# Fewer and larger loads in a windowed attention and feed-forward kernel, in a fixed order ahead of the first ones

## The chip, the cores and the metric

The kernel runs on one core of one Trainium2 chip. The metric is the device time of one execution, in microseconds (us); before the change it is 712.51 us, the median of three runs.

## The reference

Attention with 4 sink keys and a window of 128 keys, over 4 batches, 8 heads, 768 positions and 64 features a head, then a feed-forward layer from 512 to 2048 and back to 512 on all 3072 tokens. Cut to what matters:

```python
scores = np.matmul(q, k.transpose(0, 1, 3, 2)) / np.sqrt(D)
keep = is_sink | in_window                    # 4 sink keys, 128 keys of window
scores = np.where(keep, scores, -1e9)
a = np.exp(scores - scores.max(-1, keepdims=True))
a = a / (a.sum(-1, keepdims=True) + 1e-9)
x = np.matmul(a, v)                           # heads side by side: 3072 x 512
h = x @ w_in                                  # 512 -> 2048
g = np.where(h >= 1, h, np.where(h <= -1, 0.0, (h + 1) ** 2 / 4))
return g @ w_out                              # 2048 -> 512
```

The weights are 64-bit floats in memory and are decoded in the kernel from their integer words.

## The kernel before, in words

A **unit** is one head of one batch and one half of its positions (three tiles of 128 queries), 64 units in all; a **chunk** is 8 units, the rows for which a feed-forward step has 384 tokens. Chunks 0 to 3 are the first halves, 4 to 7 the second halves.

The first 16 units (two chunks) are worked as 8 **pairs** of two heads in plain 32-bit matmuls. Pair `m` has `pair_load` (L389: keys, L396, and queries, L397, by two DMAs), `pair_values` (L400: for each of two heads one DMA for its values, L404, and one for its 4 sink values, L405, into a tile `vq` that was set to zero before, L634), `pair_scores` (L412: products on PE, masked minimum on DVE, L433, exponentials on ACT, L438), `pair_sums` (L441), `early_transp` (L449), `pair_r` (L479) and `pair_av` (L463: probabilities times values on PE, L474, the scaling on DVE, L477).

The other 48 units are **split units**: queries, keys, probabilities and values are split into a rounded high part and a rest. `load` (L247 on) brings keys into `k_r` (L256) and queries into `r` (L258); ACT rounds them (L259, L262), DVE, for units 16 to 19 POOL, takes the keys' rest (L261), POOL the queries' rest `q_l` (L263). `values` (L305 on) brings a unit's values into `r` as well (L310), and its sinks into `vs_r` (L316). `r`, `k_r` and `vs_r` have one buffer each, so that queries and values take turns in `r`. `scores` ends with a small POOL step, `stat` (L289), that the row sums need.

**Order.** PE's instructions run in the order in which they are written. On the other engines and on SP's queue, from which most loads are issued, a planner that simulates the program chooses the order, except where `queue(i, on)` ties an instruction behind the one queued before it on its engine; `tc.issue_after(ins)` ties what is issued in its block behind `ins` on the engine of `ins`. Neither makes an engine wait for another. `first_pairs` (L504) writes out the first five pairs: loads of pairs 0 and 1, values of pair 0, then for each pair `m` the load of pair `m + 1`, the values of pair `m` and, after the sums of pairs 0 to 3, the fetch and the decoding of a block of weights (`weights`, L186 on; 1 MB a block; blocks 0 to 3 from SP, L199, the others from ACT's queue). A decoding is four DVE steps (L164, L170, L173, L177) and one ACT step (L174), written between the next pair's steps, and `queue` holds this order on DVE and ACT. The feed-forward of chunk 0 follows, with the other 12 blocks' decoding and pairs 5 to 7 spread over it; after that each chunk's feed-forward (`stage1`, L566, and `stage2`, L585) has the next chunk's attention spread over it.

Of the kernel before, what the change touches and what calls it, by code (L numbers as in the profile page):

```python
# [1 line left out]

# [6 lines left out]
F32 = mybir.dt.float32  # L9
F32R = mybir.dt.float32r  # L10
# [5 lines left out]
B, H, S, D = 4, 8, 768, 64  # L16
DM, DFF = 512, 2048
P = 128
NT = S // P
CT = 3  # L20
NSINK = 4
KB = P + NSINK
NCT = DM // P
QK = CT * P + P + CT * KB
# [13 lines left out]
SYNC = 4  # L38
# [11 lines left out]
def attn_ffn(ctx, tc, qk, qkp, vx, vs, par, w_in, w_out, out):  # L50
    nc = tc.nc
# [12 lines left out]
    def queue(i, on=True):  # L64
        if on:
            e = i.ins.engine
            if e in queued:
                tc.add_manual_dep(i.ins, queued[e].name, mybir.DependencyInfo(
                    mybir.DependencyClass.NoSync, mybir.DependencyReason.DATA), reason="queue")
            queued[e] = i.ins  # L70
        return i
# [57 lines left out]
    with tc.issue_after(behind):  # L129
        tsel = const.tile([44, CT], F32, name="tsel")  # L130
        nc.gpsimd.memset(tsel, 0.0)
        for r0 in (0, 32):
            r = r0 + CT * NSINK
# [16 lines left out]
    raw = {}  # L150
# [7 lines left out]
    def decode_parts(t, w, words, pin=False, on=False):  # L158

        low, x = words[..., 0], words[..., 1]  # L160
        high, rest = (t[:, :, 0], t[:, :, 1]) if len(t.shape) == 4 else (t[:, 0], t[:, 1])

        def shift():
            first = nc.vector.tensor_scalar(w, x, 3, 0x3FFFFFFF, op0=ALU.logical_shift_left, op1=ALU.bitwise_and)  # L164
            if pin:
                tc.keep_in_program_order(first)
            queue(first, on)

        def sign():
            queue(nc.vector.scalar_tensor_tensor(w, x, -0x40000000, w, op0=ALU.bitwise_and, op1=ALU.bitwise_or), on)  # L170

        def tail():
            queue(nc.vector.scalar_tensor_tensor(w, low, 29, w, op0=ALU.logical_shift_right, op1=ALU.bitwise_or), on)  # L173
            queue(nc.scalar.copy(high, w.bitcast(F32)), on)  # L174

        def rest_of():
            queue(nc.vector.tensor_tensor(rest, w.bitcast(F32), high.bitcast(F32), op=ALU.subtract), on)  # L177

        return shift, sign, tail, rest_of
# [6 lines left out]
    loaded = []  # L186

    def weights(n):

        def src(k):  # L190
            return (w_in, w_out)[k % 2][k // 2 * 2:k // 2 * 2 + 2].bitcast(I32).rearrange("j p c -> p j c")

        def fetch():
            for k in range(n, min(n + min(AHEAD if n > 2 else 1, NP // 2 - n // 2 - 1) + 1, NP)):
                if k not in raw:
                    raw[k] = wpool.tile([P, 2, 2 * DM], I32, name="w")

                    with tc.issue_after(loaded[-1]) if k < SYNC else nullcontext():
                        (nc.sync if k < SYNC else nc.scalar).dma_start(raw[k], src(k))  # L199

        def parts(on):
            j, i = n // 2 * 2, n % 2
            words = raw[n].rearrange("p j (c two) -> p j c two", two=2)
            if i:
                t = wpool.tile([P, 2, 2, DM], F32R, name="w")
                w_o[j:j + 2] = t[:, 0], t[:, 1]
            else:
                t = wi2[n // 2]
            return decode_parts(t, dec.tile([P, 2, DM], I32, name=f"bits{n % 2}"), words, pin=not on, on=on)

        def f():
            fetch()
            for g in parts(False):
                g()

        if n < WFIRST:
            return fetch, lambda: parts(True)
        return f
# [24 lines left out]
    att1 = fast.enter_context(tc.tile_pool(name="att1", bufs=1))  # L243
    att = fast.enter_context(tc.tile_pool(name="att", bufs=2))
    fast.enter_context(tc.manual_schedule(engines={mybir.EngineType.PE}))
    st = {}

    def load(u):
        b, h, t0 = u
        T = CT * P  # L250
        W = (P if t0 else -NSINK) + CT * KB
        q_l = att.tile([P, T], F32R, name="q_l")
        q_h = att.tile([P, T], F32R, name="q_h")
        k_r = att1.tile([P, P + CT * KB], F32, name="k_r")[:, :W]
        k_s = att.tile([P, P + CT * KB], F32R, name="k_s")[:, :W]
        nc.sync.dma_start(k_r, qk[b, h, t0 // CT, :, T:T + W])  # L256
        q_r = att1.tile([P, T], F32, name="r")
        nc.sync.dma_start(q_r, qk[b, h, t0 // CT, :, :T])  # L258
        nc.scalar.copy(k_s, k_r)  # L259
        eng = nc.gpsimd if units.index(u) in KL_POOL else nc.vector  # L260
        eng.tensor_tensor(k_s[D:P], k_r[D:P], k_s[D:P].bitcast(F32), op=ALU.subtract)  # L261
        nc.scalar.copy(q_h, q_r)  # L262
        nc.gpsimd.tensor_tensor(q_l, q_r, q_h.bitcast(F32), op=ALU.subtract)  # L263
        st["qk", u] = ((q_h, q_l), k_s)
# [40 lines left out]
    def values(u):  # L305
        b, h, t0 = u
        kb0 = max(t0 - 1, 0)
        nb = t0 + CT - kb0
        v_r = att1.tile([P, 4, D], F32, name="r")[:, :nb]
        nc.sync.dma_start(v_r, vx[b, h, :, kb0:kb0 + nb])  # L310
        v_s = att.tile([P, 4, 2, D], F32R, name="v_s")[:, :nb]
        i, j = h % 2, 1 - h % 2
        nc.scalar.copy(v_s[:, :, i, :], v_r)
        nc.gpsimd.tensor_tensor(v_s[:, :, j, :], v_r, v_s[:, :, i, :].bitcast(F32), op=ALU.subtract)
        vs_r = att1.tile([44, D], F32, name="vs_r")
        nc.sync.dma_start(vs_r, vs[b, h])  # L316
        vs_s = vsx[units.index(u) % 2]
        nc.scalar.copy(vs_s[0:44, i, :], vs_r)
        nc.gpsimd.tensor_tensor(vs_s[0:44, j, :], vs_r, vs_s[0:44, i, :].bitcast(F32), op=ALU.subtract)
        st["v", u] = (v_s, vs_s)  # L320
# [68 lines left out]
    def pair_load(m):  # L389

        b, h, _ = units[2 * m]
        T = CT * P
        W = CT * KB - NSINK
        q_s = att.tile([P, T], F32R, name="q_h").bitcast(F32)
        k_s = att.tile([P, P + CT * KB], F32R, name="k_s").bitcast(F32)[:, :W]
        loaded.append(nc.sync.dma_start(k_s, qkp[b, h // 2, :, T:T + W]).ins)  # L396
        nc.sync.dma_start(q_s, qkp[b, h // 2, :, 0:T])  # L397
        st["qk", m] = q_s, k_s

    def pair_values(m):  # L400
        v_s = vq[m % 2]
        for a in range(2):
            b, h, _ = units[2 * m + a]
            nc.sync.dma_start(v_s[:, :CT, a], vx[b, h, :, :CT])  # L404
            nc.sync.dma_start(v_s[:NSINK, CT, a], vs[b, h, :NSINK])  # L405

    def early_p(u):

# [54 lines left out]
    def pair_av(m):  # L463

        T = CT * P
        v_s = vq[m % 2]
        ps = ps_a.tile([P, 512], F32, name="ps_a")

        terms = [(2, 4, 1, 2), (0, 0, 2, 0), (1, 2, 2, 1), None]
        for n, t in enumerate(terms):  # L470
            for a in range(2):
                k, s0, ns, i = t or (CT, 0, 1, CT - 1)
                rhs = pt0[a][:, s0 * P:(s0 + ns) * P] if t else spn[a]
                nc.tensor.matmul(ps[a * D:a * D + D, i * P:(i + ns) * P], lhsT=v_s[:, k, a], rhs=rhs,  # L474
                                 start=(n == 0), stop=(n == len(terms) - 1))
        x = xn[:, units[2 * m][1] // 2, :]
        return lambda: queue(nc.vector.tensor_tensor(x, ps[:, :T], x, op=ALU.mult), m < H // 2)  # L477
# [63 lines left out]
    units = [(b, h, t0) for b, t0 in chunks for h in range(H)]  # L541

    def attn_steps(n):
        us = {k: units[n - k] for k in (-1, 0, 1, 2) if 0 <= n - k < len(units)}
        steps = []
        if n == NATIVE:
            steps.append((0.0, lambda: load(us[0])))
        if -1 in us:
            steps.append((0.0, lambda: load(us[-1])))
        if 1 in us and n - 1 >= NATIVE:  # L550
            steps.append((0.0, lambda: values(us[1])))
        steps += [(0.22, lambda i=i: scores(us[0], i)) for i in range(CT) if 0 in us]
        steps += [(0.43, lambda: transp(us[1]))] if 1 in us and n - 1 >= NATIVE else []
        steps += [(1.0, lambda: av(us[2]))] if 2 in us and n - 2 >= NATIVE else []
        if n in CHECK:
            steps.append((0.0, lambda: recheck(n - CHECK[0], n)))
        return steps
# [70 lines left out]

    early = ExitStack()
    dec = early.enter_context(tc.tile_pool(name="dec", bufs=1))  # L630
    vq = [dec.tile([P, CT + 1, 2, D], F32, name=f"vq{i}") for i in range(2)]
    spn = [dec.tile([P, P], F32, name=f"spn{i}") for i in range(2)]
    for t in vq + spn:
        nc.vector.memset(t, 0.0)  # L634
    p0 = [att.tile([P, CT, 260], F32, name="p").rearrange("p i c -> p (i c)") for _ in range(2)]
    pt0 = [att.tile([P, 2, CT, 2, P], F32R, name="pt").bitcast(F32).rearrange("p a i c q -> p (a i c q)")
# [4 lines left out]
    for c in range(len(chunks)):  # L641
# [12 lines left out]
        b, t0 = chunks[c]  # L654
# [17 lines left out]
    ps = ps_a.tile([P, 512], F32, name="ps_a")  # L672
# [56 lines left out]
    with tc.If(other_v > 0):  # L729
        with tc.tile_pool(name="gen", bufs=1) as gen:  # L730

            for n in range(2 * NJ):
# [3 lines left out]
                m = gen.tile([P, DM], F32, name="m")  # L736
# [3 lines left out]
            for t0 in (0, CT):  # L740
                keep = gen.tile([P, CT, S], F32, name="keep")
                kidx = gen.tile([P, S], I32, name="kidx")
                r = gen.tile([P, S], F32, name="r")
                for i in range(CT):
                    m = keep[:, i]
# [53 lines left out]
```

## Time and profile before

| | before |
|---|---|
| time, median of 3 runs | 712.51 us (712.22 to 712.81) |
| the profiled execution's own time | 713.94 us |
| its span, first to last instruction | 712.2 us |
| mean granted clock of TensorE | 0.994 |
| busy PE, DVE, ACT, POOL | 688.1, 512.9, 489.4, 296.2 us |

The span is what the trace covers; the time has what lies around it too, and an execution under the profiler is a little longer than the median. PE is TensorE's matmuls, PEld its weight loads, DVE VectorE, ACT ScalarE, POOL GpSimd, SP the engine that issues most DMAs. A busy PE counts matmuls whose ends are modelled, so a stretch in which PE is full by this count can still have it waiting a little.

### The profile page before, as it was taken

The numbers are of one execution on the slowest core, as the hardware profiler recorded it, in microseconds if no ns is written. First come the engines' busy times: TensorE is split into PE (matmuls) and PEld (weight loads), VectorE is DVE, ScalarE is ACT, GpSimd is POOL, SyncE is SP. The second block draws the span as 40 slices with busy tenths as digits, with TensorE's granted clock in tenths as the row PEclk, the third lists the DMA queues.
The fourth block names the chain that finished last, engine by engine and source line by source line (L and its number), as shares of the span: only waits on it lengthen the run. The fifth ranks groups of instructions, "written<-read, shape, count | busy, mean of one in ns | idle before, by whom it ended". The sixth has DMA issues, their size and how long they took to land.

```text
span 712.2 us, 12391 instructions
## 1 busy us (share of the span) xinstructions
PE 688.1 (97%) x3937; PEld 611.2 (86%) x3937; DVE 512.9 (72%) x1405; ACT 489.4 (69%) x1265; POOL 296.2 (42%) x509
## 2 busy tenths in 40 slices
PE   6799998999999999999999999999999999999996
PEld 4577877999999999999899898999989999989995
DVE  7978998886767768788777778778776777632221
ACT  5876666686768777786777777777766866544332
POOL 2012444754544554456564455636554444400000
PEclk9999999999999999999999999999999999999999
DMA  8845533132144333254433443334422220001001
GB/s 266 297 159 188 177 126 102 46 103 58 50 138 136 104 111 120 73 165 128 118 99 108 118 126 118 118 119 123 123 56 60 88 60 17 8 1 46 0 1 49
DMA packets 44841, 73.04 MB, mean 103 GB/s; under 512 B 13024, under 2 KB 29408, under 8 KB 44768
## 3 DMA queue, kind: packets, MB, share of 16 engines
q1 hardware_dynamic: 41504, 59.59, 27.5%
q10 hardware_dynamic: 3264, 12.58, 4.9%
q8 instruction: 33, 0.54, 0.3%
q14 instruction: 40, 0.33, 0.1%
HBM read 65.87 MB, written 6.29 MB: 101 GB/s over the span
## 4 chain that ended last, share of the span: by engine, by line
PE 73%; DVE 11%; ACT 6%; DMA 3%; POOL 2%; issue 2%; SPq 0%; ACTq 0%; POOLq 0%; DVEq 0%
PE o_ps L585 30%; PE h_ps L566 30%; PE ps_a L383 4%; PE ps_a L277 4%; PE ps_a L336 2%; DVE bits L170 1%; DMA again<-w_in 1%; DVE bits L173 1%; DVE p L298 1%; ACT p L284 1%; DMA w<-w_in 1%; DVE g L575 1%; DVE gl L577 1%; POOL q_l L263 1%; PE ps_a L474 1%
## 5 line engine op out<-in xcount | busy, mean ns | idle before, releaser
L566 PE MATMUL h_ps<-x,wi 128*128 128x384 f32 x1536 | 310.5, 341 | 0.0
L566 PEld LDWEIGHTS h_ps<-x,wi 128*128 128x128 f32 x1536 | 264.3, 189 | 9.8 <-issue 1.5
L585 PE MATMUL o_ps<-w,gh 128*128 128x512 f32 x768 | 243.9, 398 | 0.0
L585 PE MATMUL o_ps<-w,gl 128*128 128x512 f32 x384 | 151.2, 394 | 0.9 <-DVE gl L577 0.9
L585 PEld LDWEIGHTS o_ps<-w,gh 128*128 128x128 f32 x768 | 134.1, 188 | 16.5 <-issue 1.7
L575 DVE SCALAR_TENSOR_TENSOR g<-g,h_ps 128x384 f32<-128x384 f32 x128 | 70.4, 550 | 63.9 <-ACT g L574 62.2
L573 ACT ACTIVATE g<-h_ps,half 128x384 f32<-128x384 f32 x128 | 73.9, 578 | 58.0 <-PE h_ps L566 56.9
L263 POOL TENSOR_TENSOR q_l<-r,q_h 128x384 fp32r<-128x384 f32 x48 | 50.7, 1056 | 132.1 <-ACT q_h L262 123.2
L576 ACT CAST gh<-g 128x384 fp32r<-128x384 f32 x128 | 65.6, 512 | 57.3 <-DVE g L575 56.8
L585 PEld LDWEIGHTS o_ps<-w,gl 128*128 128x128 f32 x384 | 72.0, 188 | 18.6 <-DVE gl L577 1.3
L577 DVE TENSOR_TENSOR gl<-g,gh 128x384 fp32r<-128x384 f32 x112 | 68.6, 612 | 25.3 <-ACT gh L576 24.3
L284 ACT ACTIVATE p<-p,peak 128x260 f32<-128x260 f32 (+1 forms) x144 | 71.4, 496 | 17.5 <-DVE peak L281 16.8
L261 DVE TENSOR_TENSOR k_s<-k_r,k_s 64x524 fp32r<-64x524 f32 (+1 forms) x44 | 46.4, 1054 | 40.0 <-ACT k_s L259 39.9
L574 ACT ACTIVATE g<-g 128x384 f32<-128x384 f32 x128 | 66.9, 523 | 2.1
L281 DVE CUSTOM_DVE_ANT_0 p<-ps_a,m 128x260 f32<-128x260 f32 (+1 forms) x144 | 56.6, 409 | 15.9 <-PE ps_a L277 15.1
L347 POOL TENSOR_SCALAR_AFFINE_SELECT pt<-pt 128x384 fp32r<-128x384 f32 (+1 forms) x96 | 51.0, 531 | 18.2 <-DVE pt L340 16.3
L298 DVE CUSTOM_DVE_ANT_0 p<-p,stat 128x128 f32<-128x128 f32 x128 | 55.4, 477 | 0.0
L345 POOL TENSOR_SCALAR_AFFINE_SELECT pt<-pt 128x384 fp32r<-128x384 f32 (+1 forms) x96 | 50.4, 525 | 7.1 <-ACT pt L339 3.0
L577 POOL TENSOR_TENSOR gl<-g,gh 128x384 fp32r<-128x384 f32 x16 | 22.6, 1415 | 69.0 <-ACT gh L576 65.5
L383 PEld LDWEIGHTS ps_a<-pt,v_s 128*128 128x128 f32 x304 | 46.6, 188 | 2.2
L383 PE MATMUL ps_a<-pt,v_s 128*128 128x256 f32 (+1 forms) x304 | 47.0, 275 | 0.0
L277 PE MATMUL ps_a<-k_s,q_h 128*128 128x260 f32 (+1 forms) x144 | 40.0, 278 | 0.9 <-DVE sk L342 0.9
(147 smaller groups left out, 977.2 us busy)
## 6 DMA issues: line engine op xcount, KB each, us to landing
r<-qk SPq DMA_DIRECT2D x48, 192.0 KB
k_r<-qk SPq DMA_DIRECT2D x32, 262.0 KB
again<-w_in SPq DMA_DIRECT2D x16, 512.0 KB
again<-w_out SPq DMA_DIRECT2D x16, 512.0 KB
w<-w_in ACTq DMA_DIRECT2D x6, 1024.0 KB
w<-w_out ACTq DMA_DIRECT2D x6, 1024.0 KB
out<-o SPq DMA_DIRECT2D x23, 256.0 KB
r<-vx SPq DMA_DIRECT2D x32, 128.0 KB
```

Source lines behind the costliest of these rows:

```text
L263: nc.gpsimd.tensor_tensor(q_l, q_r, q_h.bitcast(F32), op=ALU.subtract)
L277: nc.tensor.matmul(ps[:, lo:260], lhsT=q[:, i * P:(i + 1) * P], rhs=k_s[:, c0:c0 + 260 - lo], start=(j == 0), stop=(j == len(qs) - 1))
L284: nc.scalar.activation(p[:, i, lo:260], p[:, i, lo:260], AF.Exp, bias=peak_i, scale=-1.0, accum_out=stat[:, i:i + 1])
L298: nc.vector.tensor_tensor_reduce(out=own, in0=own, in1=p[:, i, 0:P], scale=r, scalar=0.0, op0=ALU.add, op1=ALU.add, accum_out=stat[:, i:i ...
L383: nc.tensor.matmul(z, lhsT=w, rhs=y, start=(n == 0), stop=(n == len(mms) - 1))
L566: nc.tensor.matmul(h_ps[:, :T], lhsT=w_i[j][:, w, ct * P:(ct + 1) * P], rhs=x[:, y, ct], start=(ct == 0 and n == 0), stop=(ct == NCT - 1 a ...
L573: nc.scalar.activation(g, h_ps[:, :T], AF.Relu, bias=half, scale=0.5)
L574: nc.scalar.activation(g, g, AF.Square)
L575: nc.vector.scalar_tensor_tensor(g, g, 1.0, h_ps[:, :T], op0=ALU.min, op1=ALU.max)
L576: nc.scalar.copy(gh, g)
L577: (nc.gpsimd if row0 == GL_POOL else nc.vector).tensor_tensor(gl, g, gh.bitcast(F32), op=ALU.subtract)
L585: nc.tensor.matmul(o_ps[tt], lhsT=gg[:, tt * P:(tt + 1) * P], rhs=w_o[j][:, w], start=(j == 0 and n == 0), stop=(j == NJ - 1 and n == 2))
```

## The change

A pair's queries and keys come in one DMA into one tile `qk_s`, and its two heads' values in one DMA into `vq`, whose layout is now head, tile, feature; `vq` has no place for sinks, is not set to zero, and the sinks' product takes the first tile of keys with probabilities that are zero but for four rows. A split unit's queries and keys come in one DMA into one tile `qk_r`, and its values have a tile `v_r` of their own. The pairs' loads and the first four weight blocks' are tied one behind the other on SP's queue (pairs 0 to 5), and a split unit's loads are tied behind the last pair's load that was written before them. The matmuls, their sizes and all other arithmetic stay.

```diff
-                    with tc.issue_after(loaded[-1]) if k < SYNC else nullcontext():
-                        (nc.sync if k < SYNC else nc.scalar).dma_start(raw[k], src(k))
+                    queue((nc.sync if k < SYNC else nc.scalar).dma_start(raw[k], src(k)), k < SYNC)
...
-        q_h = att.tile([P, T], F32R, name="q_h")
-        k_r = att1.tile([P, P + CT * KB], F32, name="k_r")[:, :W]
-        k_s = att.tile([P, P + CT * KB], F32R, name="k_s")[:, :W]
-        nc.sync.dma_start(k_r, qk[b, h, t0 // CT, :, T:T + W])
-        q_r = att1.tile([P, T], F32, name="r")
-        nc.sync.dma_start(q_r, qk[b, h, t0 // CT, :, :T])
+        qk_r = att1.tile([P, QK], F32, name="qk_r")[:, :T + W]
+        qk_s = att.tile([P, QK], F32R, name="qk_s")[:, :T + W]
+        with tc.issue_after(loaded[-1]):
+            nc.sync.dma_start(qk_r, qk[b, h, t0 // CT, :, :T + W])
+        q_r, k_r = qk_r[:, :T], qk_r[:, T:]
+        q_h, k_s = qk_s[:, :T], qk_s[:, T:]
...
-        v_r = att1.tile([P, 4, D], F32, name="r")[:, :nb]
-        nc.sync.dma_start(v_r, vx[b, h, :, kb0:kb0 + nb])
+        v_r = att1.tile([P, 4, D], F32, name="v_r")[:, :nb]
+        with tc.issue_after(loaded[-1]):
+            nc.sync.dma_start(v_r, vx[b, h, :, kb0:kb0 + nb])
...
-        nc.sync.dma_start(vs_r, vs[b, h])
+        with tc.issue_after(loaded[-1]):
+            nc.sync.dma_start(vs_r, vs[b, h])
...
-        q_s = att.tile([P, T], F32R, name="q_h").bitcast(F32)
-        k_s = att.tile([P, P + CT * KB], F32R, name="k_s").bitcast(F32)[:, :W]
-        loaded.append(nc.sync.dma_start(k_s, qkp[b, h // 2, :, T:T + W]).ins)
-        nc.sync.dma_start(q_s, qkp[b, h // 2, :, 0:T])
-        st["qk", m] = q_s, k_s
+        qk_s = att.tile([P, QK], F32R, name="qk_s").bitcast(F32)[:, :T + W]
+        loaded.append(queue(nc.sync.dma_start(qk_s, qkp[b, h // 2, :, :T + W]), m < H // 2 + 2).ins)
+        st["qk", m] = qk_s[:, :T], qk_s[:, T:]
...
-        for a in range(2):
-            b, h, _ = units[2 * m + a]
-            nc.sync.dma_start(v_s[:, :CT, a], vx[b, h, :, :CT])
-            nc.sync.dma_start(v_s[:NSINK, CT, a], vs[b, h, :NSINK])
+        b, h, _ = units[2 * m]
+        queue(nc.sync.dma_start(v_s, vx[b, h:h + 2, :, :CT].rearrange("a p t d -> p a t d")), m < H // 2 + 2)
...
-                k, s0, ns, i = t or (CT, 0, 1, CT - 1)
+                k, s0, ns, i = t or (0, 0, 1, CT - 1)
-                nc.tensor.matmul(ps[a * D:a * D + D, i * P:(i + ns) * P], lhsT=v_s[:, k, a], rhs=rhs,
+                nc.tensor.matmul(ps[a * D:a * D + D, i * P:(i + ns) * P], lhsT=v_s[:, a, k], rhs=rhs,
...
-    vq = [dec.tile([P, CT + 1, 2, D], F32, name=f"vq{i}") for i in range(2)]
+    vq = [dec.tile([P, 2, CT, D], F32, name=f"vq{i}") for i in range(2)]
-    for t in vq + spn:
+    for t in spn:
         nc.vector.memset(t, 0.0)
```

## Rows read from the trace of the kernel before

**Rows 1.** The page, part 1: busy us (share of the span) xinstructions of each engine.

```profile
PE 688.1 (97%) x3937; PEld 611.2 (86%) x3937; DVE 512.9 (72%) x1405; ACT 489.4 (69%) x1265; POOL 296.2 (42%) x509
```

**Rows 2.** The chain of work that ended last, in order of time, in the stretch 0 to 18 us: start us, us, what.

```profile
2.63 0.20 DVE x L106
2.83 0.13 DVE x L108
...
3.04 0.13 DVE x L115
...
4.94 6.29 DMA w<-w_in
```

**Rows 3.** The timeline of SP's queue, 0 to 60 us: start us, us, queue, line, operation, out<-in, count. The last row is the second half of the last pair's load.

```profile
1.24 0.42 SPq L396 DMA_DIRECT2D k_s<-qkp  x1
1.71 0.42 SPq L397 DMA_DIRECT2D q_h<-qkp  x1
...
59.96 0.57 SPq L397 DMA_DIRECT2D q_h<-qkp  x1
```

**Rows 4.** The page, part 6 (DMA issues: out<-in, queue, operation, count, KB each), asked for in full.

```profile
w<-w_in SPq DMA_DIRECT2D x2, 1024.0 KB
...
k_s<-qkp SPq DMA_DIRECT2D x8, 196.0 KB
q_h<-qkp SPq DMA_DIRECT2D x8, 192.0 KB
vq<-vx SPq DMA_DIRECT2D x16, 96.0 KB
```

**Rows 5.** Stretches of one us each: us, then busy time of PE, PEld, DVE, ACT, POOL (instructions), granted clock, mean busy share of the 16 DMA engines, GB/s.

```profile
6.00:7.00 1.00, 1.00 (x8) 0.56 (x4) 1.00 (x5) 0.86 (x4) 0.89 (x6) 1.00 0.88 118
7.00:8.00 1.00, 0.77 (x3) 0.18 (x1) 1.00 (x7) 0.28 (x1) 0.87 (x6) 1.00 0.90 340
```

**Rows 6.** The timeline of DVE, 0 to 18 us: start us, us, engine, line, operation, out<-in, shapes, count, and in brackets the idle time before it and what ended it.

```profile
0.96 1.03 DVE L634 MEMSET vq<- 128x512 f32 x2 [0.96 <-PEq L792]
...
10.05 0.19 DVE L446 RECIPROCAL stat<-stat 128x6 f32<-128x6 f32 x1
11.25 0.69 DVE L164 TENSOR_SCALAR bits<-w 128x1024 int32<-128x1024 int32 x1 [1.01 <-DMA w<-w_in]
...
13.54 0.42 DVE L433 CUSTOM_DVE_ANT_0 pt<-o_ps,m1n 128x260 f32<-128x260 f32 x1
...
14.24 1.22 DVE L173 SCALAR_TENSOR_TENSOR bits<-w,bits 128x1024 int32<-128x1024 int32 x1
```

**Rows 7.** The timeline of PE, 0 to 18 us, in the columns of group 6.

```profile
4.83 1.20 PE L422 MATMUL o_ps<-k_s,q_h 64*128 64x128 f32 x5 [4.83 <-DMA q_h<-qkp]
...
11.48 1.23 PE L422 MATMUL o_ps<-k_s,q_h 64*128 64x128 f32 x5
...
12.51 0.64 PE L422 MATMUL o_ps<-k_s,q_h 64*128 64x260 f32 x1
...
12.95 0.64 PE L422 MATMUL ps_a<-k_s,q_h 64*128 64x260 f32 x1
```

**Rows 8.** The chain of waits again, in the stretch 30 to 135 us: two pairs' last small products, and the first split units.

```profile
34.92 1.48 PE ps_a L486 x12
36.40 2.17 PE ps_a L474 x16
...
106.72 0.81 PE ps_a L486 x12
...
110.14 1.45 PE ps_a L474 x16
...
119.72 1.03 POOL k_s L261
...
120.82 0.24 POOL stat L289
...
124.02 3.36 PE h_ps L566 x12
...
129.46 2.08 PE h_ps L566 x12
```

**Rows 9.** Waits between 124 and 600 us, summed: the row of ACT for the queries' load, then the two largest of PE: who waited for what, us in total, times, longest us.

```profile
ACT q_h L262 <- DMA r<-qk: 7.5, 9, 1.9
...
PE ps_a L277 <- DVE sk L342: 0.9, 3, 0.4
PE o_ps L585 <- DVE gl L577: 0.9, 1, 0.9
```

**Rows 10.** Timelines of ACT, POOL and PE around the split units, in the columns of group 6.

```profile
79.61 0.52 ACT L259 CAST k_s<-k_r 128x392 fp32r<-128x392 f32 x1 [0.74 <-PE ps_a L422]
...
118.38 1.26 POOL L263 TENSOR_TENSOR q_l<-r,q_h 128x384 fp32r<-128x384 f32 x1 [1.58 <-ACT q_h L262]
...
121.71 0.87 PE L336 MATMUL ps_a<-ident,p 128*128 128x128 f32 x3 [1.95 <-DVE p L296]
...
123.88 1.98 POOL L261 TENSOR_TENSOR k_s<-k_r,k_s 64x392 fp32r<-64x392 f32 x1 [1.19 <-ACT k_s L259]
...
406.32 1.02 POOL L263 TENSOR_TENSOR q_l<-r,q_h 128x384 fp32r<-128x384 f32 x1 [3.00 <-ACT q_h L262]
...
415.71 0.51 ACT L262 CAST q_h<-r 128x384 fp32r<-128x384 f32 x1 [0.72 <-DMA r<-qk]
```

More of the change, by code (lines that the diff above doesn't have):

```diff
@@ L1 @@
-from contextlib import ExitStack, nullcontext
+from contextlib import ExitStack
 import concourse.bass as bass
```

## The prediction, made before the change was run

> **What bounds the kernel now.** I read the page's busy times first: PE is busy for 97% of the span [rows 1], so what doesn't reach PE's queue is worth little, and a load matters only where somebody on the way to PE stands still for it. Then I read the chain of waits from the start. While the first five pairs run there is no feed-forward: DVE masks, reads scores and decodes weights, PE follows, and what leaves DVE's queue earlier moves all behind it. In that stretch the chain has one load of weight: block 0 of the weights, issued at 4.94 and landed 6.29 us later [rows 2]. DVE's timeline says what that costs: the sums of pair 0 start at 10.05 and take 0.19, the first decoding step starts at 11.25, and 1.01 us before it are idle, ended by that load [rows 6]. Later the chain is PE and DVE in turn. Between 124 and 600 us PE's two largest waits are 0.9 us each, for DVE; no load is among them. ACT does stand still for a load there, 7.5 us in 9 waits for a split unit's queries [rows 9], but off the path.
>
> **The change part by part.** The sum is made on the profiled execution (713.94 us, of which 712.2 are span and 1.74 lie around it) and carried to the median of 712.51, which is 1.43 lower; a difference is taken to be the same in both.
>
> *Block 0 lands earlier.* Before, SP issues parameters, keys and queries of two pairs, and four loads for the values ahead of it. An issue takes 0.42 us and the next follows 0.47 after the last [rows 3]. Merged, three issues (two pairs, one for the values) stand ahead, so the block's turn comes at 1.24 + 3 x 0.47 = 2.65 instead of 4.94: 2.3 us earlier at most. But the DMA engines were occupied meanwhile: the bytes ahead stay, 388 KB for each of two pairs and 192 KB of values [rows 4], and only their rate can improve. Between 6 and 7 us, when values move in short pieces, the engines are 0.88 busy at 118 GB/s; a microsecond later 0.90 at 340 [rows 5]. The 0.197 MB of values take 1.67 us at the first rate and 0.58 at the second, so at most 1.1 us come free there; new pieces are three times as long, so I take two thirds of it, 0.7. Landing then lies between 11.23 - 2.3 = 8.9 and 11.23 - 0.7 = 10.5 (11.2 if the rate doesn't move). DVE can use it from 10.24 on, so of the 1.01 idle 0.7 to 1.01 go by the likely landings; the bounds are 0 and 1.01.
>
> *What is late next.* The decoding's first two steps, which end when the reads behind them start, then end 0.7 to 1.0 sooner, and DVE's order has the four reads of pair 1's first scores next, then step L173. These wait for PE: its matmuls for pair 1 begin at 11.48 behind the transposes of pair 0, which no load holds up, and the third score's last pass begins at 12.51 and the next products at 12.95 [rows 7]. So the third read, now at 13.54, can't start before about 13.0, and L173, now at 14.24 [rows 6], moves to about 13.7. **Gain: 0.5 us**, not 1.01. From there the loop of decodings runs as before, and its later blocks had landed in time.
>
> *No clearing of `vq`.* The two fills take 1.03 us of DVE from 0.96 on [rows 6], before the parameters land; the masks need these. What can slide forward into the room are three steps that need no parameters and now stand behind them, 0.20 + 0.13 + 0.13 us [rows 2]. That pulls the first score reads, and with them the transposes and pair 1's matmuls, so it adds to the 0.5. The planner decides; between 0 and 0.46 I take 0.3. The first matmul's load is no bar: PE had its operands at 4.83 [rows 7], and one load that is issued at 1.24 isn't later than two of which the second left at 1.71 [rows 3].
>
> *Order of the first loads.* Up to block 1 the order before is already the written one; tying it gives 0. Block 3 now waits behind the values of pair 2, which wait for pair 0's product; what covers it is the decoding of blocks 1 and 2, which comes first; were that cover gone, it would cost what is left of one landing, 6.29 us at most [rows 2]. I take 0.
>
> *Split units' loads later.* Units 16 and later may now load only after the last pair's, whose second half was issued at 59.96 [rows 3]. Unit 16's keys are first used at 79.61, after a wait for PE, not for the load [rows 10]. 19 us cover it; cost 0. The cost if that cover went would be the landing of one load.
>
> *One tile for queries and keys, one for values.* The joint tile is free only when the slowest reader is done, POOL's `q_l`. In the steady stretch that ends at 406.32 + 1.02 = 407.3, and ACT takes the next queries at 415.71 [rows 10]: 8 us for one landing. In exchange values no longer hold up queries, and the 7.5 us of ACT's waits should go [rows 9]. ACT has room, PE's own waits there are two of 0.9; I take 0, bounds 0 to 1.8 gained. 80 fewer DMAs leave SP (4 for each of 8 pairs, one for each of 48 units), none on the path: 0.
>
> *The clock.* Two groups of a pair's small products run 1.48 + 2.17 us at 34.92 and 36.40, and 0.81 + 1.45 at 106.72 and 110.14 [rows 8]: the first two fall into a stretch at the lower of the two levels, 1.2 GHz, that follows gaps in PE's work. It costs 1.39 us; an earlier start might move or remove it. I take 0. [...]
>
> Sum: -0.5 - 0.3 = -0.8 us: 713.1 for a profiled execution, **711.7** for the median. Own range: 712.5 (neither term) to 711.0 (1.01 + 0.46).
>
> **The rivals.**
> 1. *Nothing arrives* (712.5): the values' rate doesn't improve and the planner leaves the masks where they are, or the gain is lost in a later wait. For it: bytes are the same. Against: three issues and the short pieces do go.
> 2. *The clock stretch at 34 us goes with the gaps before it*: 711.7 - 1.4 = 710.3. Against it: the loop there is DVE's, and its gaps on PE stay.
> 3. *PE's stall at the first split units goes.* PE waits 1.95 us for unit 16's probabilities, until 121.71 [rows 10]; behind it twelve products take 3.36 instead of 2.08 us, at the lower clock [rows 8]. The cause is an order: `stat` at 120.82 stands on POOL behind unit 18's `q_l` (118.38, 1.26) and key rest (119.72, 1.03) [rows 8, 10]. With other loads the planner may put it first, or that work earlier. 1.95 + 1.28 and a little of the next group, some 3.7 in all: 711.7 - 3.7 = 708.0. Against it: unit 18's tiles come free at the same point as before, with unit 16's scores.
> 4. **Slower:** *the same place gets worse.* Queries and keys now become ready together, and if POOL does both at the duration that its key rest has at 123.88 (1.98) [rows 10] in place of 1.26 + 1.03, `stat` comes 1.7 us later, PE stands 1.7 longer, and a longer lower clock adds about as much again as it now costs, 1.28 to 1.7: 711.7 + 3.0 to 3.4, **714.9**. It decides against the forecast once `stat` is over 0.8 us later against its scores than now. For it: all orders off PE are chosen anew, and this place has no slack.
>
> **How the numbers follow.** About 0.2% (1.4 us) is what a measurement can tell from no change. Forecast (-0.8): 0.42. Rival 1: 0.10. Rival 2: 0.13. Rival 3: 0.15. Rival 4: 0.20, as a planner that sees other loads can do harm anywhere in DVE's stretch, too. Faster by over 1.4 us: rivals 2 and 3 and a little of the forecast, if the waits of 0.9 go as well, 0.32. Slower: rival 4, 0.20. The rest, 0.48, is no change. The range goes from rival 3 to rival 4: 708.0 to 715.0; it leaves out only a stall that grows further or several gains at once.
>
> **What would show it.** Right: the first decoding step within 0.1 us of the end of pair 0's sums; L173 at about 13.4; three SP issues between parameters and block 0; ACT's row of waits for queries gone; the first feed-forward product, and all up to the first split units, some 0.8 us earlier. Wrong: a DVE idle time ended by block 0 again; a new wait of DVE or PE for a load; PE's wait before the transposes near 121 us gone or longer; another place of the lower clock.

## The result, and the profile after

The changed kernel is **slower**: 720.63 us (719.78 to 722.83, 4 runs) against 712.37 of the kernel before beside it; ratio 1.012, 95% interval 1.0094 to 1.0146. On another chip it came to 718.03 (717.13 to 720.61, 6 runs) against 712.45: 1.0078, 1.0057 to 1.0098. So it costs some 6 to 8 us. The profiled execution took 719.78, span 718.1.

TensorE's 3937 matmuls stand in the same order in both traces, so their start times can be subtracted one by one. The **lag** of the changed kernel (after less before, us) then says where the time goes. Each column is the matmul that ran at that time before:

| kernel | 18 | 82 | 87 | 135 | 264 | 443 | 531 | 705 us |
|---|---|---|---|---|---|---|---|---|
| after | -0.4 | -1.9 | +3.2 | +2.0 | +2.0 | +2.7 | +5.7 | +5.7 |
| after, second chip | -0.3 | -1.2 | +4.1 | +2.8 | +2.8 | +2.5 | +3.8 | +3.8 |
| values late (e1) | -0.3 | -1.2 | -1.2 | -1.3 | -1.3 | +0.4 | +3.6 | +3.6 |
| queries first (e7) | -0.3 | -1.0 | +4.3 | +2.6 | +2.6 | +0.3 | +0.4 | +0.4 |
| both (e6) | -0.4 | -0.7 | -0.7 | -0.8 | -0.7 | -3.3 | -3.1 | -3.1 |
| pairs' part (e3) | -0.3 | -0.3 | -0.3 | -0.6 | -0.6 | +2.0 | +3.0 | +3.0 |
| split units' part (e4) | +1.0 | +1.8 | +7.2 | +6.6 | +6.6 | +8.5 | +11.7 | +11.7 |

Each line is one profiled execution, and a stretch at the lower clock can be in one and not in the other; the medians decide on the sizes, the lag on the places. There are two: one jump of 5.1 to 5.3 us at 82 to 87 us, part of which comes back by 135, and a slow loss between 264 and 531.

**The start went as foreseen.** SP's timeline: three issues between the parameters and the first weight block, the block at 2.65 instead of 4.94 [rows 2].

```profile
1.24 0.90 SPq L396 DMA_DIRECT2D qk_s<-qkp  x2
2.18 0.43 SPq L402 DMA_DIRECT2D vq<-vx  x1
2.65 0.47 SPq L198 DMA_DIRECT2D w<-w_in  x1
```

DVE's timeline after (columns of group 6): the first decoding step follows the sums with no wait for a load, 10.33 instead of 11.25, and L173 starts at 13.88 instead of 14.24 [rows 6]. In between DVE waits 0.36 for PE.

```profile
10.05 0.19 DVE L443 RECIPROCAL stat<-stat 128x6 f32<-128x6 f32 x1
10.33 0.69 DVE L164 TENSOR_SCALAR bits<-w 128x1024 int32<-128x1024 int32 x1
...
13.18 0.43 DVE L430 CUSTOM_DVE_ANT_0 pt<-o_ps,m1n 128x260 f32<-128x260 f32 x1 [0.36 <-PE h_ps L419]
...
13.88 1.22 DVE L173 SCALAR_TENSOR_TENSOR bits<-w,bits 128x1024 int32<-128x1024 int32 x1
```

**The first place, 82 to 87 us.** SP's timeline after, 57 to 75 us. The split units' loads come behind the last pair's; unit 17's values (66.55) and sinks (67.01) are issued when POOL is done with unit 16's:

```profile
59.68 0.48 SPq L310 DMA_DIRECT2D v_r<-vx  x1
...
66.55 0.35 SPq L310 DMA_DIRECT2D v_r<-vx  x1
67.01 0.31 SPq L317 DMA_DIRECT2D vs_r<-vs  x1
```

ACT's timeline after, with two rows of ACT's own DMA queue. The value and sink copies of units 16 and 17 (L313, L319) now stand among the pairs' work. The second pair of them finds its data not there: 3.25 us and 0.63 idle, beside two weight blocks of 1 MB each that were issued at 66.10 and 66.88. Behind them stand a pair's exponentials and, between two of these, a step of the feed-forward (L571):

```profile
64.67 0.35 ACT L313 CAST v_s<-v_r 128x192 fp32r<-128x192 f32 x1 [0.60 <-DMA v_r<-vx]
...
66.10 0.37 ACTq L198 DMA_DIRECT2D w<-w_in  x1
66.88 0.39 ACTq L198 DMA_DIRECT2D w<-w_out  x1
...
71.29 0.35 ACT L313 CAST v_s<-v_r 128x192 fp32r<-128x192 f32 x1 [3.25 <-DMA v_r<-vx]
72.27 0.24 ACT L319 CAST vsx<-vs_r 44x64 fp32r<-44x64 f32 x1 [0.63 <-DMA vs_r<-vs]
...
72.92 0.51 ACT L571 ACTIVATE g<-g 128x384 f32<-128x384 f32 x1
```

DVE then waits 4.18 us for that step, and the decodings slip:

```profile
73.53 0.56 DVE L572 SCALAR_TENSOR_TENSOR g<-g,h_ps 128x384 f32<-128x384 f32 x1 [4.18 <-ACT g L571]
```

PE's timeline shows where this arrives, at 83.81, and the six products behind it at the lower clock (1.2 GHz; the granted clock is 0.53 from 86 to 88 us):

```profile
83.81 0.83 PE L419 MATMUL ps_a<-qk_s 64*128 64x128 f32 x4 [2.69 <-DVE peak L430]
...
86.08 2.25 PE L563 MATMUL h_ps<-x,wi 128*128 128x384 f32 x6
```

In the kernel before these copies ran at 121.66 and 130.95.

A part comes back near 121 us: PE's wait for unit 16's probabilities is there as before, 1.95 us [rows 10], but the twelve products behind it are not at the lower clock: the granted clock is 0.50 from 124 to 126 us before and 1.00 from 124 to 130 after. PE's timeline, first before, then after:

```profile
123.82 3.56 PE L566 MATMUL h_ps<-x,wi 128*128 128x384 f32 x12
```

```profile
126.09 2.25 PE L563 MATMUL h_ps<-x,wi 128*128 128x384 f32 x12
```

So it is in both runs of the changed kernel and in e7, whose lag falls by 1.2 to 1.7 us between 87 and 135.

**The second place, 264 to 531 us.** PE's waits over the whole span, summed. It stood at 0.9 in 3 waits before [rows 9]: a score's product waits for a buffer in PSUM, the memory that PE writes to. DVE frees it when it reads the sinks' part from it (L343), a step that comes behind its scaling of the sinks' probabilities into `sk` (L300; L301 before), which is called `sk` from here on:

```profile
PE ps_a L276 <- DVE sk L343: 3.7, 4, 1.8
```

DVE's instructions between 150 and 680 us by shape (count, busy us, mean ns, idle before): first before, then after.

```profile
L298 DVE CUSTOM_DVE_ANT_0 p<-p,stat 128x128 f32<-128x128 f32 x120 | 52.3, 481 | 0.0
...
L261 DVE TENSOR_TENSOR k_s<-k_r,k_s 64x524 fp32r<-64x524 f32 x32 | 33.8, 1056 | 32.0 <-ACT k_s L259 32.0
...
L301 DVE TENSOR_TENSOR sk<-p,stat 128x12 f32<-128x12 f32 x32 | 13.9, 435 | 0.0
```

```profile
L297 DVE CUSTOM_DVE_ANT_0 p<-p,stat 128x128 f32<-128x128 f32 x122 | 59.5, 532 | 0.7
...
L260 DVE TENSOR_TENSOR qk_s<-qk_r,qk_s 64x524 fp32r<-64x524 f32 x32 | 22.4, 701 | 16.2 <-ACT qk_s L258 15.0
L300 DVE TENSOR_TENSOR sk<-p,stat 128x12 f32<-128x12 f32 x32 | 17.9, 559 | 0.0
```

The same work got other durations: the keys' rest is faster (1056 to 701 ns), normalising (L297; 481 to 532) and `sk` (435 to 559) slower. What runs beside them moved. POOL and DVE before, at one unit: POOL takes the queries' rest at 522.49, DVE's keys' rest (522.98) takes 1.09 beside it, and `sk` at 525.55 takes 0.17.

```profile
522.49 1.02 POOL L263 TENSOR_TENSOR q_l<-r,q_h 128x384 fp32r<-128x384 f32 x1 [4.08 <-ACT q_h L262]
```

```profile
522.98 1.09 DVE L261 TENSOR_TENSOR k_s<-k_r,k_s 64x524 fp32r<-64x524 f32 x1 [1.73 <-ACT k_s L259]
...
525.55 0.17 DVE L301 TENSOR_TENSOR sk<-p,stat 128x12 f32<-128x12 f32 x1
```

The same unit after, POOL, DVE and PE: the queries' rest starts 0.46 after the keys' rest (525.48 against 525.02), where it started 0.49 ahead of it; all that POOL does next is later against DVE, the second and third normalising steps take 0.6, and `sk` takes 1.45 beside the rests of sinks and values (528.72, 529.04). The score's product waits 1.83.

```profile
525.48 1.13 POOL L262 TENSOR_TENSOR q_l<-qk_r,qk_s 128x384 fp32r<-128x384 f32 x1 [4.61 <-ACT qk_s L261]
...
528.72 0.35 POOL L320 TENSOR_TENSOR vsx<-vs_r,vsx 44x64 fp32r<-44x64 f32 x1
529.04 0.74 POOL L314 TENSOR_TENSOR v_s<-v_r,v_s 128x256 fp32r<-128x256 f32 x1
529.73 0.51 POOL L348 TENSOR_SCALAR_AFFINE_SELECT pt<-pt 128x384 fp32r<-128x384 f32 x1
```

```profile
525.02 0.70 DVE L260 TENSOR_TENSOR qk_s<-qk_r,qk_s 64x524 fp32r<-64x524 f32 x1 [1.31 <-ACT qk_s L258]
...
527.76 0.61 DVE L297 CUSTOM_DVE_ANT_0 p<-p,stat 128x128 f32<-128x128 f32 x1
...
528.83 1.45 DVE L300 TENSOR_TENSOR sk<-p,stat 128x12 f32<-128x12 f32 x1
...
531.37 0.28 DVE L343 TENSOR_TENSOR sk<-ps_a,sk 12x128 fp32r<-12x128 f32 x1
```

```profile
531.79 0.36 PE L276 MATMUL ps_a<-qk_s 128*128 128x260 f32 x1 [1.83 <-DVE sk L343]
```

The loss comes in four units. Where the kernel before is at 318, 356, 443 and 528 us, the lag rises by 1.3, 0.9, 0.9 and 3.2, and in these units `sk` takes 0.98, 0.69, 0.69 and 1.45, where it took 0.16 to 0.17 before. A long `sk` is not a loss everywhere: two in the kernel before take 1.46 (at 581.36 and 592.46) with no wait of PE over 0.3 behind them. It costs where PE is next in need of the buffer. Between these units the lag falls again by some 2 us, where the kernel before has waits of its own.

What moved them is the order of two roundings on ACT, which e6, e7 and e8 turn. Before, queries are rounded ahead of keys in 45 of 48 split units; after, keys first in all 48.

### The profile page after: what moved, and what is told of

Read it like the earlier page. It is cut to its first block, busy times and chain, and to the rows that moved or that the text cites. A ratio compares the mean times of both kernels' runs of the same rounds, so it can differ in the third digit from the quotient of the medians.

```text
span 718.1 us, 12210 instructions
## 1 busy us (share of the span) xinstructions
PE 688.7 (96%) x3937; PEld 612.1 (85%) x3937; DVE 516.9 (72%) x1403; ACT 487.0 (68%) x1265; POOL 289.5 (40%) x509
## 4 chain that ended last, share of the span: by engine, by line
PE 61%; DVE 12%; ACT 9%; issue 6%; DMA 5%; POOL 4%; SPq 0%; ACTq 0%; POOLq 0%; DVEq 0%
PE h_ps L563 26%; PE o_ps L582 25%; PE ps_a L384 3%; PE ps_a L276 3%; DMA again<-w_in 2%; ACT p L283 2%; PE ps_a L337 1%; DVE p L297 1%; DVE bits L170 1%; DMA again<-w_out 1%; DVE bits L173 1%; ACT g L570 1%; DVE gl L574 1%; DVE g L572 1%; ACT g L571 1%
## 5 line engine op out<-in xcount | busy, mean ns | idle before, releaser
L574 DVE TENSOR_TENSOR gl<-g,gh 128x384 fp32r<-128x384 f32 x112 | 74.3, 663 | 28.1 <-ACT gh L573 26.3
L262 POOL TENSOR_TENSOR q_l<-qk_r,qk_s 128x384 fp32r<-128x384 f32 x48 | 54.7, 1139 | 83.5 <-ACT qk_s L261 83.2
L571 ACT ACTIVATE g<-g 128x384 f32<-128x384 f32 x128 | 67.0, 523 | 2.2
L297 DVE CUSTOM_DVE_ANT_0 p<-p,stat 128x128 f32<-128x128 f32 x128 | 62.4, 531 | 0.7
L348 POOL TENSOR_SCALAR_AFFINE_SELECT pt<-pt 128x384 fp32r<-128x384 f32 (+1 forms) x96 | 51.1, 546 | 5.8 <-DVE pt L341 5.8
L228 POOL COPY again<-peak 1x1 f32<-1x1 f32 x32 | 6.3, 197 | 113.7 <-DVE peak L280 108.3
L346 POOL TENSOR_SCALAR_AFFINE_SELECT pt<-pt 128x384 fp32r<-128x384 f32 (+1 forms) x96 | 47.9, 514 | 7.9 <-ACT pt L340 4.6
L350 POOL TENSOR_TENSOR sp<-sk,tsel 44x384 fp32r<-44x384 f32 (+1 forms) x48 | 37.1, 773 | 18.5 <-DVE sk L343 17.8
```

The source lines that it names most:

```text
L297: nc.vector.tensor_tensor_reduce(out=own, in0=own, in1=p[:, i, 0:P], scale=r, scalar=0.0, op0=ALU.add, op1=ALU.add, accum_out=stat[:, i:i ...
L571: nc.scalar.activation(g, g, AF.Square)
L574: (nc.gpsimd if row0 == GL_POOL else nc.vector).tensor_tensor(gl, g, gh.bitcast(F32), op=ALU.subtract)
```

## The experiments

Each was timed beside the kernel before, so that ratios compare better than medians from different chips. Theory A: the values' copies on ACT. Theory B: the joint tile of loaded queries and keys. Theory C: the fixed order of the pairs' loads. Then D: the order of the two roundings, and E: the joint tiles as such.

**e1, values behind the exponentials.** Each split unit's copies of values and sinks are tied behind its own last exponential.

```diff
+        with tc.issue_after(st["exp", u]):     # the unit's last exponential
             nc.scalar.copy(v_s[:, :, i, :], v_r)
...
+        with tc.issue_after(st.pop(("exp", u))):
             nc.scalar.copy(vs_s[0:44, i, :], vs_r)
```

> The changed kernel, in which the two ACT copies that take in a split unit's values and sinks are tied on ACT behind that unit's own last exponential; loads and tiles as changed. Theory A (the loss near 70 us is ACT standing for the early values of units 16 and 17): the 5.1 us that PE falls behind between 78 and 87 us are gone, the time is 715.5 (714.5 to 716.7), and ACT has no wait for v_r before 100 us. Theory B (the joint tile of queries and keys, read by three engines, is what costs): nothing changes there, 719.5 to 721.5. Theory C (the fixed order of the pairs' loads costs): the same as B, 719.5 to 721.5.

Measured 716.25 (714.15 to 717.65) against 712.17; ratio 1.0053, 1.0032 to 1.0073. The jump at 82 us is gone, the slow loss stays. A holds, for the first place only.

**e2, values in the joint tile.**

```diff
-        v_r = att1.tile([P, 4, D], F32, name="v_r")[:, :nb]
+        v_r = att1.tile([P, QK], F32, name="qk_r")[:, :nb * D].rearrange("p (t d) -> p t d", d=D)
```

> The changed kernel, but a split unit's values come into the one buffer of queries and keys (as they took turns with queries before), so that they can't be loaded early; the sinks' loads stay early. Theory A: most of the 5.1 us are back, as ACT's waits of 3.25 and 0.60 us for v_r go and the one of 0.63 for vs_r stays; 716 (715 to 718), less what turns in one buffer cost later. Theory B: the buffer is fuller, 720 to 723. Theory C: 719.5 to 721.5.

Measured 725.92; ratio 1.0197, 1.0174 to 1.0219, worse than any case expected. It takes away the first jump and puts many small ones in the steady stage: one buffer for everything makes ACT wait for loads. ACT's waits between 124 and 600 us:

```profile
ACT qk_s L258 <- DMA qk_r<-qk: 19.9, 20, 2.9
...
ACT v_s L313 <- DMA qk_r<-vx: 7.9, 13, 1.7
```

So the values' own tile is worth its place; the run says nothing for B as it was meant.

**e3, the pairs' part alone.** Split units load as before, through `k_r` and `r`, untied, but round into two slices of one tile `qk_s`, which they share with the pairs.

```diff
-        with tc.issue_after(loaded[-1]):
-            nc.sync.dma_start(qk_r, qk[b, h, t0 // CT, :, :T + W])
-        q_r, k_r = qk_r[:, :T], qk_r[:, T:]
+        nc.sync.dma_start(k_r, qk[b, h, t0 // CT, :, T:T + W])
+        q_r = att1.tile([P, T], F32, name="r")
+        nc.sync.dma_start(q_r, qk[b, h, t0 // CT, :, :T])
```

> Only the pairs' part of the change (one load for queries and keys, one for both heads' values, fixed order with the weights); split units load keys, queries and values as before, untied, with r and k_r. Theory A and B: the start's gain stays (0.35 by the earlier first weights, 1.4 by the lower clock near 35 us that is not met) and the loss is not there: 710.6 (710 to 712.5). Theory C: 716 or more.

Measured 714.22 (712.82 to 716.89); ratio 1.0025, 1.0012 to 1.0039. No theory had it. No loss up to 264 us, so not C; no joint load, so not B; and yet the slow loss. What it shares with the change is the joint *rounded* tile, and ACT rounds keys first in 48 of 48 units.

**e4, the split units' part alone.** The pairs keep two loads for queries and keys, into two slices of `qk_s`, and the order and values of before; the split units are those of the change.

```diff
-        q_s = att.tile([P, T], F32R, name="q_h").bitcast(F32)
-        k_s = att.tile([P, P + CT * KB], F32R, name="k_s").bitcast(F32)[:, :W]
+        qk_s = att.tile([P, QK], F32R, name="qk_s").bitcast(F32)[:, :T + W]
+        q_s, k_s = qk_s[:, :T], qk_s[:, T:]
```

> Only the split units' part (one load into a joint tile, values with a tile of their own, tied behind the pairs' loads); pairs load as before with two and four loads. Theory A and B: the loss without the start's gain, 720.5 (719 to 723), and A has ACT waiting over 3 us for v_r near 70 us again. Theory C: 712.5 (711.5 to 713.5).

Measured 724.57 (720.67 to 727.02); ratio 1.0164, 1.0136 to 1.0193, above all that was expected. Both places are there (+5.3 at 82, with ACT waiting 3.33 for `v_r`, and +5.1 between 264 and 531), and it starts 1.0 late besides. The start and the rest of its excess over the change were not followed.

**e6, e7 and e8: the order of the roundings.** e7 puts the queries' rounding first in the changed kernel; e6 does so on top of e1; e8 puts the keys' first in the kernel before.

```diff
-        nc.scalar.copy(k_s, k_r)
-        eng = nc.gpsimd if units.index(u) in KL_POOL else nc.vector
-        eng.tensor_tensor(k_s[D:P], k_r[D:P], k_s[D:P].bitcast(F32), op=ALU.subtract)
-        nc.scalar.copy(q_h, q_r)
+        first = nc.scalar.copy(q_h, q_r).ins
         nc.gpsimd.tensor_tensor(q_l, q_r, q_h.bitcast(F32), op=ALU.subtract)
+        with tc.issue_after(first):
+            nc.scalar.copy(k_s, k_r)
+        eng = nc.gpsimd if units.index(u) in KL_POOL else nc.vector
+        eng.tensor_tensor(k_s[D:P], k_r[D:P], k_s[D:P].bitcast(F32), op=ALU.subtract)
```

> The changed kernel with the split units' value copies on ScalarE behind their own exponentials (as in the experiment that did this alone, 716.25 us) and, new, the queries' rounding ahead of the keys' rounding in every split unit. Theory D: in the kernel before ScalarE rounds the queries first in 45 of 48 split units, in every kernel with the joint tile of rounded queries and keys the keys first in 48 of 48; GpSimd's queries' rest then runs some 0.6 us later, no longer beside VectorE's keys' rest (1.06 us each before, 0.70 after) but up to VectorE's normalising of p and sk (0.481 and 0.435 before, 0.53 and 0.58 after), whose end frees the PSUM buffer for the next score. With the order back, the steady stage's 4.9 us of lag go: 711.3 (710.5 to 712.5), keys' rest near 1.05 again and normalising near 0.48. Theory E, the joint tiles as such (buffers free later, other order of transfers) cost it: 716 (715 to 717.5).

> The changed kernel with only the queries' rounding put ahead of the keys' rounding; the values' copies stay where the change put them. D: 720.6 less some 4.4, 716.2 (715 to 717.5), TensorE's lag of 5.1 us at 83 us still there. E: 720.6 (719.5 to 722).

> The kernel before, nothing of the change, with the queries' rounding tied behind the keys' in every split unit. D: 712.2 and some 4, 716 (714.5 to 717.5), with the keys' rest at 0.70 us and the normalising at 0.53. E: 712.2 (711.5 to 713.2).

> The changed kernel once more, as the measure for the others on this chip: 720.6 (719 to 722) by every theory.

Measured on one chip, the kernel before at 712.45 (29 runs):

| | median, us | ratio to before, 95% |
|---|---|---|
| after again | 718.03 | 1.0078, 1.0057 to 1.0098 |
| e7, queries first | 714.34 | 1.0033, 1.0017 to 1.0049 |
| e6, queries first and values late | **711.04** | 0.9978, 0.9967 to 0.9989 |
| e8, before with keys first | 713.89 | 1.0021, 1.0009 to 1.0033 |

The order gives 3.69 of the change's loss back (718.03 to 714.34), the late values 3.30 more, and with both the change is faster than the kernel before by 0.22%. D holds in its sign and E falls: e6 has both joint tiles. Of D's numbers only e6's came out; the changed kernel itself is 2.6 lower on this chip than on the first, e7 is 0.7 below D's range for it, and e8 lies between the ranges of D and E. DVE's rows in e6, in the columns above, and PE's largest waits between 124 and 600 us:

```profile
L299 DVE CUSTOM_DVE_ANT_0 p<-p,stat 128x128 f32<-128x128 f32 x121 | 52.9, 482 | 0.0
...
L263 DVE TENSOR_TENSOR qk_s<-qk_r,qk_s 64x524 fp32r<-64x524 f32 x32 | 35.3, 1102 | 26.8 <-ACT qk_s L261 26.8
...
L302 DVE TENSOR_TENSOR sk<-p,stat 128x12 f32<-128x12 f32 x32 | 13.8, 432 | 0.0
```

```profile
PE ps_a L277 <- DVE sk L347: 0.6, 2, 0.4
```

e8 shows the order at work with nothing of the change, but at 1.4 us (0.6 to 2.4), not 4. Its rows say what is missing. DVE, then POOL:

```profile
526.03 0.28 DVE L302 TENSOR_TENSOR sk<-p,stat 128x12 f32<-128x12 f32 x1
```

```profile
526.82 0.73 POOL L315 TENSOR_TENSOR v_s<-r,v_s 128x256 fp32r<-128x256 f32 x1 [0.55 <-ACT v_s L314]
```

There values still come in `r`, and ACT waits 0.74 for them here, so POOL's values' rest comes after `sk`, which takes 0.28. With a tile of their own they are early, and that rest runs beside `sk`: 1.45 after. The other runs bear this out for that unit: in all five kernels with keys first and an own tile for values (after, after again, e1, e4, e5) `sk` takes 1.44 to 1.45 there and PE waits 1.83 to 1.85; in e3 and e8, with keys first and values in `r`, 0.28 and 0.65; in e6 and e7 `sk` takes 0.17 and PE has no wait over 0.3 there. So the order and the early values together make the larger loss, and e3's slow loss is the order without early values, as e8's is.

**e9, e11, e12 and e5.** e9 is e3 with the queries' rounding first. e11 is e6 with this edit; e12 has it for all split units; e5 is the changed kernel without `tc.issue_after(loaded[-1])` at the split units' three loads.

```diff
-        nc.gpsimd.tensor_scalar(stat[:, CT:2 * CT], stat[:, 0:CT], 1.0e-9, None, op0=ALU.add)
+        eng = nc.vector if units.index(u) in KL_POOL else nc.gpsimd
+        eng.tensor_scalar(stat[:, CT:2 * CT], stat[:, 0:CT], 1.0e-9, None, op0=ALU.add)
```

> The pairs' part alone (as in the run of that name, 714.22 us: split units load as before, but round queries and keys into one joint tile), with the queries' rounding now ahead of the keys'. D, the joint tile acts through the order of ScalarE's two roundings alone: 711.9 (711 to 712.7), that is the kernel before less the 0.35 us that the first weight block brings. If the joint tile, or the fixed order of the pairs' loads, costs by itself: 714.2 (713 to 715.5).

> The changed kernel with late values and queries first (711.04 us), and the small step that adds 1e-9 to the row sums on VectorE instead of GpSimd for units 16 to 19. It tests the prediction's third rival: TensorE waits 2.1 us for unit 16's probabilities at 121.2, as this step (120.19) stands on GpSimd behind the queries' rest (117.72, 1.30) and the keys' rest (119.09, 1.01). If that order makes the stall, normalising can start at 119.9 in place of 120.7: TensorE's wait falls to 1.3 or less, and with the lower clock behind it (twelve products 3.22 in place of some 2.1) 0.8 to 2 us are gained: 709.6 (708.5 to 710.4). If the keys' rest on GpSimd holds VectorE up anyway: 711.0 (710.3 to 712).

> The same for all 48 split units: the step leaves GpSimd (44 of them at some 0.3 us) and comes to VectorE (some 0.15 each, 7 us in all, off the path while TensorE is the bound). As the run with units 16 to 19 alone if only the stall at 121 us matters: 709.6 (708 to 711). If VectorE's queue is short at the places where scores wait for a PSUM buffer: slower than that run by 1 to 3 us.

> The changed kernel without the ties that put the split units' loads behind the pairs'. The planner then issues units 16 to 18's loads as numbers 7 to 18 on the queue, ahead of the weights, and their value copies stand on ScalarE at places 16 and 31 in place of 109 and 119. If it is the values' own tile that lets the copies come early, and the tie only sets how early: a stall for them or for the weights in the first 40 us, 716 to 722, without the 5.1 us at 83. If it is the tie itself that brings the copies and their late data together: 714.5 (713 to 716), the changed kernel less those 5.

Measured on one chip, the kernel before at 712.67 (33 runs): e9 713.38 (1.0014, 1.0000 to 1.0028), e11 710.85 (0.9975, 0.9962 to 0.9987), e12 715.07 (1.0034, 1.0021 to 1.0047), e5 714.58 (1.0036, 1.0020 to 1.0053).

*e9* lies in the range of its second expectation, 0.7 above the first's. Its trace loses 0.3 us between 264 and 705, where e3 lost 3.6, but its ratio falls only from 1.0025 to 1.0014, with intervals that overlap. Whether the pairs' part costs something by itself stays open, between 0 and 2.0 us.

*e11* gains nothing on e6 by its ratio (0.9975 to 0.9978), as its second expectation had it, though not for that reason: PE's and POOL's timelines show that the wait that ends at 119.39 is 1.11 in place of 2.1, but PE then stands 2.00 until 130.18 for `gl` (L579, the rest of a feed-forward activation), which comes behind the rests of values and sinks in a full queue on POOL.

```profile
119.39 0.66 PE L342 MATMUL ps_a<-ident,p 128*128 128x128 f32 x2 [1.11 <-DVE p L298]
...
130.18 0.50 PE L587 MATMUL o_ps<-w,gl 128*128 128x512 f32 x1 [2.00 <-POOL gl L579]
```

```profile
128.49 0.69 POOL L325 TENSOR_TENSOR vsx<-vs_r,vsx 44x64 fp32r<-44x64 f32 x1
129.14 0.98 POOL L579 TENSOR_TENSOR gl<-g,gh 128x384 fp32r<-128x384 f32 x1
```

*e12* is slower than e11 by 4.2 us, more than the 1 to 3 expected: with that step on DVE everywhere, products wait for `sk` 2.5 us in 4 waits, against 0.6 in 2 in e6. DVE is short in places, although it is busy for only 75% of e12's span.

*e5* comes out at its second expectation, 714.5, and has no jump at 82 us: a split unit's values are issued at 4.19, and ACT's copies at 14.00 and 20.13 wait 0.38 at most. SP's and ACT's timelines:

```profile
4.19 0.48 SPq L308 DMA_DIRECT2D v_r<-vx  x1
```

```profile
14.00 0.35 ACT L311 CAST v_s<-v_r 128x192 fp32r<-128x192 f32 x1 [0.38 <-DMA v_r<-vx]
...
20.13 0.34 ACT L311 CAST v_s<-v_r 128x192 fp32r<-128x192 f32 x1
```

So the tie, which made the loads late, and the values' own tile, which let the planner set their copies early, cost the 5 us together: with the tie alone (e2), the tile alone (e5) or neither (e3) the jump is not there. e5 keeps the slow loss, as it should.

## Why the prediction was wrong

The forecast was 711.7 with a chance of 0.20 for slower; the result lies 5.6 us above its range. By its steps:

*Block 0 lands earlier*: right in mechanism, 0.36 us in place of 0.5 (L173 at 13.88 in place of 14.24). The bound named, PE's products for pair 1, is the one that the trace shows.

*No clearing of `vq`*: 0 in place of 0.3. The first score read stays at 5.65; the planner left the small steps behind the parameters.

*Order of the first loads*: 0, as forecast; the lag of e3, which has this order, stays at -0.3 from 18 to 87 us.

***Split units' loads later: "19 us cover it; cost 0"* failed.** It cost about 5 us in TensorE's lag, of which the clock near 121 us gave some back, and 3.3 in medians (e7 to e6). The cover was taken from the first use of unit 16's keys at 79.61 [rows 10]. But three loads were moved, and the first use of the values was not looked up: it is a copy on ACT, an engine that runs in order, and where it stands is the planner's choice. With a tile of their own the values could come at once, so the planner set the copies ahead of pair work; the landing of unit 17's, 4.7 us (66.55 to 71.29) beside 2 MB of weights, made them a stop for ACT, DVE and PE in turn.

***One tile for queries and keys: "I take 0, bounds 0 to 1.8 gained"* failed**, and its sign was excluded without a reason. The 7.5 us of ACT's waits for queries did go [rows 9]. What was not priced is an order: two tiles came free one after the other, a joint one comes free at once, and the keys' rounding, which is written first, goes first. I take the release as the reason; that the joint tile turns the order is shown (e3), why is argued. The order costs 3.7 us in the changed kernel (after again to e7) and 1.4 in the kernel before (e8). The gain that the bounds allowed does exist, and the order hid it: in e6 the lag falls by 2.6 us between 264 and 443, where the kernel before has waits of 0.85, 0.45 and 0.31 (401.46, 432.60, 435.35; 1.6 in all) that e6 does not have. In e9, whose split units load as before, this gain is not there.

*The clock*: at 34 to 38 us the profiled run after has a granted clock of 1.00 where before had 0.57, and its lag falls by 1.5 us between 18 and 82. That is what rival 2 had named. But e8, which changes nothing there, has 1.00 too, and e3, which has the earlier start, 0.57 again. Not to count on it was right. First before, then after:

```profile
34.00:38.00 4.00, 3.76 (x27) 2.84 (x29) 2.95 (x4) 2.99 (x8) 0.00 (x0) 0.57 0.43 121
```

```profile
34.00:38.00 4.00, 3.84 (x43) 2.70 (x43) 3.91 (x11) 2.90 (x9) 0.00 (x0) 1.00 0.07 9
```

*Rivals 3 and 4*: the wait behind `stat` stayed at 1.95 us; only the lower clock behind it went. The slower case came, by a planner that set other orders, but not at the place that had been named. Rival 3's price of 3.7 us was too high in any case: e11 takes away a good part of that stall and meets POOL's `gl` 11 us later.

## What to carry to other kernels

A load that is moved or given its own buffer moves its first consumer as well: look up on which in-order engine that consumer stands, and what is queued behind it, before calling the load covered. Two tiles merged into one lose the order in which they came free, and with it who runs beside whom; when durations of unchanged instructions differ between two traces, look at what the other engine did in that time. And a stall taken away is worth no more than the distance to the next queue that is full.

## What the hardware showed beside this

**VectorE and GpSimd hold each other up.** The keys' rest, one instruction, takes 0.70 us with GpSimd idle, and also when the queries' rest starts 0.46 behind it, but 1.09 when the queries' rest started 0.49 ahead. The queries' rest takes 1.02 in the second case and 1.13 in the first, so the later one pays. `sk` takes 0.16 to 0.17 alone and 1.45 beside the rests of sinks and values, and ends at 530.28, when GpSimd's run of work beside it ends (530.24). A tenth of a microsecond decides: in the kernel before `sk` takes 0.16 where a select on GpSimd starts 0.01 ahead of it (at 534.75), and 0.47, to the end of that select, where one starts 0.12 ahead (at 484.70). The Trainium skill, SBUF — State Buffer, section "Who interferes with whom", says that a VectorE instruction with two inputs in SBUF contends with a GpSimd instruction that reads SBUF. These rows agree: the stretched ones have two inputs in SBUF. So does the counterpart: between 150 and 680 us of the changed kernel `g<-g,h_ps`, with one input in PSUM, takes 0.53 to 0.56 in all 103 rows, and `gl<-g,gh` of the same size, with both in SBUF, 0.54 to 1.85. What carries the contention no run here takes apart.

**One stall, two clocks.** The same wait of 1.83 and 1.85 us before a score at 531 is followed by a granted clock of 0.83 (part of the stretch at 1.2 GHz) in one profiled run of the changed kernel and of 1.00 (2.4 GHz) in the other (us, then busy time of PE, PEld, DVE, ACT, POOL, clock, DMA share, GB/s; first chip, then second):

```profile
530.00:535.00 5.00, 3.21 (x16) 3.14 (x17) 4.37 (x14) 2.41 (x8) 1.07 (x2) 0.83 0.11 28
```

```profile
530.00:535.00 5.00, 3.52 (x22) 3.43 (x23) 4.28 (x13) 2.72 (x8) 1.02 (x2) 1.00 0.09 26
```

In the first the lag grows by 1.6 us more. The Trainium skill, TensorE: Matmul & The Clock Gate, "Part 1: The HAM clock gate", says that at its start one kernel ran different numbers of matmuls at the low rate in different runs. These two runs show such a difference after a stall in the middle of a kernel. The kernel before spread from 710.5 to 715.1 us over the chips used, so that several runs of each kernel were needed to see 1.4.
